# Scores on two 64-row tiles and outputs with sums on two 64-column tiles, in a windowed attention with sinks followed by a gated feed-forward layer

## The chip, the cores and the metric

The kernel runs on one core of a Trainium2 chip. The metric is device time in microseconds (us) of one execution. TensorE multiplies on a 128x128 array and writes PSUM, VectorE and ScalarE read PSUM and write SBUF, GpSimd (POOL) works in SBUF and issues some of the loads, SyncE (SP) issues the others.

## The reference

Four batches, eight heads, 768 positions, head width 64. Each query sees the first four positions (the sinks) and the last 128 up to itself. What follows is a gated feed-forward layer over the 512 values of a position.

```python
scores = scale * np.matmul(q, k.transpose(0, 1, 3, 2))
keep = is_sink | in_window            # pos < 4, or 0 <= rel < 128
scores = np.where(keep, scores, -1000000000.0)
a = np.exp(scores - np.max(scores, axis=-1, keepdims=True))
a = a / (np.sum(a, axis=-1, keepdims=True) + 1e-09)
attn = np.matmul(a, v)                # then x = attn as (3072, 512)
gate = np.maximum(x @ w_gate, 0.0)    # 512 -> 1536
out = (gate * (x @ w_val)) @ w_out    # 1536 -> 512
```

## The kernel before

**Attention.** A unit is a pair of heads (p = 0 to 3) of one batch. Keys are cut into blocks j of 124 positions; a block's 128 key columns are its 124 positions and the four sinks in front, so each block of keys meets a stretch of at most 255 queries. The steps of a unit: `load_kq` and `load_v` load k, q and v; `cast` turns k and q into bf16 on GpSimd (`kn`, `qn`); `T` transposes them on TensorE (`tk`, `tq` in PSUM) and copies the results to `kT` and `qz`. `qz` holds two copies of the queries with the other head's 64 rows zero, so that a 128-row matmul gives one head's scores. `S(gi)` makes the scores of a group of key blocks (`sps`), ScalarE takes the exponential into `ee`, VectorE multiplies with a 0/1 mask. `V(part, oab)` multiplies `ee` with `vn`, in which each head's 64 value columns have 64 columns of ones beside them: rows 0 to 63 of `ops` are the output, row 64 and those below it the sum of exponentials. ScalarE copies `ops` to `oab`.

**Normalisation.** Units of batches 1 to 3 (kind F, all 768 rows) go through `norm`: the sums leave by DMA to DRAM and come back as a 128x12 tile, VectorE takes the reciprocals some chunks later, these go to DRAM and come back as a broadcast `R` over 64 partitions, and again some chunks later VectorE multiplies `oab` by `R` into `xT` (`tick` counts the chunks). Batch 0 is cut into three kinds of units, A (252 rows), B (248) and C (268); they go through `norm0`, which transposes the sums out of PSUM on VectorE in 32x32 blocks, takes the reciprocal of one column per block and transposes back.

**Feed-forward.** `chunk(b, c0, n, m)` makes 128 of the 1,536 hidden values for n positions: four matmuls for the gate (`gp`), ScalarE's relu (`gs`), four for the values (`vp`), VectorE's product into `hT`. `ffn2` multiplies `hT` with `wo`, twelve matmuls of 512 columns per 128 positions, issued a few at a time behind later chunks. There are 108 chunks: 36 in batch 0 (three blocks) and 24 in each later batch (two blocks of 384).

**Order.** The order on every engine is the program order, written by hand. `unit_stages` lists the attention stages, `want` says how many of them stand ahead of a chunk. Two PSUM slots (`ps_at`) serve the transposes, scores and outputs in turn; three serve `gp` and `vp`, one serves `op`. Batch b's chunks need `xT` of all four units of that batch.

## Time and profile before

| what | value |
|---|---|
| time, median of 3 runs | 314.46 us (313.69 to 315.67) |
| the profiled execution | 312.14 us |
| its span, first to last instruction | 310.4 us |
| mean granted TensorE clock, share of 2.4 GHz | 0.984 |
| TensorE busy | 259.5 us (84%) |
| VectorE busy | 167.5 us (54%) |
| ScalarE busy | 163.2 us (53%) |
| GpSimd busy | 93.7 us (30%) |

Busy times are sums over all instructions of an engine; a share of the span is an average over stretches with different limits. In the rows below, a name with L and a number is a line of the kernel before; `x4` behind a group is its count of instructions; PEld is TensorE's weight load, which runs beside its matmuls.

### The profile page before, as it was taken

How to read it: one execution, taken by the hardware profiler on the slowest of the kernel's cores; microseconds unless marked ns; L12 is line 12 of the kernel's file. 1: busy time of each engine (PE TensorE's matmuls, PEld its weight loads, DVE VectorE, ACT ScalarE, POOL GpSimd, SP SyncE). 2: the span in 40 equal slices, each digit the busy share in tenths (PEclk: the TensorE clock that was granted, in tenths of full speed). 3: DMA queues.
4: the chain of work that ended last, by engine and by line, in shares of the span. 5: the costliest groups of instructions: out<-in, count | busy, mean ns of one | idle time of the engine just before them, and what ended most of it. 6: DMA issues, size and time to landing. Idle time of an engine off the chain costs nothing.

```text
span 310.4 us, 5251 instructions
## 1 busy us (share of the span) xinstructions
PE 259.5 (84%) x1868; PEld 168.2 (54%) x1868; DVE 167.5 (54%) x340; ACT 163.2 (53%) x300; POOL 93.7 (30%) x159
## 2 busy tenths in 40 slices
PE   1545856466798997749999999999999999999995
PEld 0333744354686765516666666666666555555552
DVE  4488667768765757544647473746454352222210
ACT  5553667445478875515566657565554333333321
POOL 7756247245595454230405050503000000000000
PEclk9999999989799999989999999999999999999999
DMA  5799997855898778391919373524312301000002
GB/s 134 140 219 202 222 236 128 130 116 117 128 151 133 186 88 145 85 201 46 171 63 188 68 150 85 64 85 29 87 36 88 84 35 37 34 34 36 34 34 101
DMA packets 55585, 33.75 MB, mean 109 GB/s; under 512 B 34428, under 2 KB 51708, under 8 KB 55560
## 3 DMA queue, kind: packets, MB, share of 16 engines
q1 hardware_dynamic: 25368, 25.59, 29.1%
q0 software_dynamic: 29104, 7.57, 24.8%
q10 hardware_dynamic: 1088, 0.26, 0.4%
q8 instruction: 14, 0.23, 0.3%
q14 instruction: 11, 0.09, 0.1%
HBM read 34.55 MB, written 6.44 MB: 132 GB/s over the span
## 4 chain that ended last, share of the span: by engine, by line
PE 55%; ACT 0%; issue 0%; ACTq 0%
PE op L411 18%; PE vp L398 15%; PE gp L392 15%; PE ops L248 3%; PE sps L232 3%; PE tk L188 1%; PE tq L195 1%; ACT ot L415 0%; ACTq L415 0%
## 5 line engine op out<-in xcount | busy, mean ns | idle before, releaser
L400 DVE TENSOR_TENSOR hT<-gs,vp 128x384 bf16<-128x384 f32 (+3 forms) x108 | 54.6, 506 | 72.2 <-PE vp L398 55.8
L392 PE MATMUL gp<-xT,wg 128*128 128x384 bf16 (+3 forms) x432 | 82.6, 315 | 4.5 <-DVE xT L364 4.5
L398 PE MATMUL vp<-xT,wv 128*128 128x384 bf16 (+3 forms) x432 | 82.7, 315 | 2.9 <-ACT gs L395 2.1
L411 PE MATMUL op<-wo,hT 128*128 128x512 bf16 x288 | 79.0, 383 | 0.0
L395 ACT ACTIVATE gs<-gp 128x384 f32<-128x384 f32 (+3 forms) x108 | 49.2, 455 | 41.2 <-PE gp L392 40.5
L398 PEld LDWEIGHTS <-wv 128*128 128x128 bf16 x432 | 43.3, 100 | 29.5 <-issue 8.6
L238 DVE TENSOR_TENSOR ee<-ee,msk 128x1006 bf16<-128x1006 bf16 (+6 forms) x52 | 38.6, 742 | 32.5 <-ACT ee L236 32.4
L236 ACT ACTIVATE ee<-sps 128x1006 bf16<-128x1006 f32 (+6 forms) x52 | 47.1, 906 | 14.7 <-PE sps L232 14.3
L392 PEld LDWEIGHTS <-wg 128*128 128x128 bf16 x432 | 40.1, 100 | 18.9
L151 POOL DMA_DIRECT2D vn<-in_v_dram x32 | 26.3, 825 | 71.8 <-PE ops L248 67.7
L411 PEld LDWEIGHTS <-hT 128*128 128x128 bf16 x288 | 28.4, 99 | 23.0 <-issue 0.6
L248 PE MATMUL ops<-ee,vn 128*128 128x248 bf16 (+9 forms) x264 | 28.2, 246 | 13.5 <-ACT qz L200 7.5
L248 PEld LDWEIGHTS <-vn 128*128 128x128 bf16 x264 | 22.6, 101 | 23.0 <-issue 13.8
L232 PE MATMUL sps<-qz,kT 128*128 128x251 bf16 (+6 forms) x136 | 27.5, 258 | 7.6 <-ACT qz L200 2.4
L252 ACT COPY oab<-ops 65x752 f32<-65x752 f32 (+1 forms) x24 | 19.0, 794 | 21.1 <-PE ops L248 21.0
L364 DVE TENSOR_TENSOR xT<-oab,R 64x768 bf16<-64x768 f32 x24 | 23.9, 996 | 11.2 <-DMA R<-rcp_tmp 10.9
L200 ACT COPY qz<-tq 64x768 bf16<-64x768 bf16 (+2 forms) x24 | 14.0, 584 | 24.8 <-DVE qz L200 24.6
L188 PE MATMUL tk<-ident,kn 128*128 128x128 bf16 (+2 forms) x112 | 11.5, 240 | 16.4 <-POOL kn L163 13.7
L232 PE MATMUL sps<-qz,kTs 128*128 128x248 bf16 (+3 forms) x104 | 25.0, 263 | 0.0
L415 ACT COPY ot<-op 128x512 f32<-128x512 f32 x24 | 14.0, 584 | 18.3 <-PE op L411 18.3
L191 ACT COPY kT<-tk 128x768 bf16<-128x768 bf16 (+3 forms) x24 | 15.1, 629 | 15.5 <-PE tk L188 15.4
L188 PEld LDWEIGHTS <-kn 128*128 128x128 bf16 (+2 forms) x112 | 8.7, 110 | 21.7 <-POOL kn L163 16.0
(61 smaller groups left out, 189.9 us busy)
## 6 DMA issues: line engine op xcount, KB each, us to landing
out_dram<-ot SPq DMA_DIRECT2D x24, 256.0 KB, 2.3
kf<-in_k_dram SPq DMA_DIRECT2D x24, 192.0 KB, 4.1
qf<-in_q_dram SPq DMA_DIRECT2D x24, 192.0 KB, 4.4
R<-rcp_tmp SPq DMA_DIRECT2D x12, 384.0 KB, 4.1
vn<-in_v_dram POOLq DMA_DIRECT2D x24, 96.0 KB, 3.6
wg<-in_moe_w_gate_dram POOLq DMA_DIRECT2D x4, 384.0 KB, 7.4
wv<-in_moe_w_val_dram POOLq DMA_DIRECT2D x4, 384.0 KB, 9.8
wo<-in_moe_w_out_dram POOLq DMA_DIRECT2D x3, 512.0 KB, 6.6
```

The costliest lines, as they stand in the source:

```text
L151: eng.dma_start(out=dst[:, o + j0:o + j0 + nj, h, 0:64], in_=bass.AP(src.tensor, src.offset + 124 * j0 * D, [[D, 128], [124 * D, nj], [1, ...
L188: nc.tensor.transpose(ps[:, t * kp:(t + 1) * kp], kn[s][0:kp, self.no + t, :, :].rearrange("p h d -> p (h d)"), ident[0:kp, 0:kp])
L232: nc.tensor.matmul(out=ps[:, h, c:c + w], lhsT=self.kw(j), rhs=qz[s][:, h, self.zo + qa:self.zo + qa + w], start=True, stop=True)
L236: nc.scalar.activation(x, ps[:, :, 0:c], Act.Exp, bias=0.0, scale=scale)
L238: nc.vector.tensor_tensor(x, x, bc(msk[:, m0:m0 + c], 2), op=Alu.mult)
L248: nc.tensor.matmul(out=ps[:, h, qa - q0:qa - q0 + w], lhsT=vn[s][:, self.vo + j, h, :], rhs=ee[s][:, gi, h, c:c + w], start=i == 0, stop=i ...
L364: nc.vector.tensor_tensor(xTs[b][64 * h:64 * h + 64, p, :], oab[0:64, h, :], R[:, h, :], op=Alu.mult)
L392: nc.tensor.matmul(out=gp[:, 0:n], lhsT=wg[:, ko, m * 128:(m + 1) * 128], rhs=x[:, ko, c0:c0 + n], start=ko == 0, stop=ko == KO - 1)
L395: nc.scalar.activation(gs[:, 0:n], gp[:, 0:n], Act.Relu, bias=0.0, scale=1.0)
L398: nc.tensor.matmul(out=vp[:, 0:n], lhsT=wv[:, ko, m * 128:(m + 1) * 128], rhs=x[:, ko, c0:c0 + n], start=ko == 0, stop=ko == KO - 1)
L400: nc.vector.tensor_tensor(hT[:, m, c0:c0 + n], gs[:, 0:n], vp[:, 0:n], op=Alu.mult)
L411: nc.tensor.matmul(out=op, lhsT=hTs[b][:, m, t * 128:(t + 1) * 128], rhs=wo[:, m, :], start=m == 0, stop=m == FM - 1)
```

## The change

- Scores: `qz` becomes `qT` with both heads' queries once. Head h's scores come from rows 64h to 64h+63 of the array, the two heads one behind the other in the order and into two PSUM banks.
- Outputs and sums: `ops` holds the outputs of head 0 in partitions 0 to 63 and of head 1 in 64 to 127, and the sums likewise in its other half. The sums come from matmuls with a tile of ones. All of these are 64 columns wide.
- Normalisation: every unit goes through one `norm`, like `norm0` before, and the product reads the output from PSUM. The DRAM round trip, the copies to `oab` and the counting of chunks are gone.
- Batch 0 has two kinds of units, L (376 rows) and M (392), and two blocks of chunks, so there are 96 chunks.
- Three staging buffers and three `vn`; one DMA for both heads of k or q; the sink rows of `vn` are copied by VectorE; `PLAN` replaces the numbers in `want`.

```diff
-    "A": dict(q0=0, n=252, ...),  "B": dict(q0=252, n=248, ...),  "C": dict(q0=500, n=268, ...)
+    "L": dict(q0=0, n=376, q=(0, 128, 3), k=(0, 96, 4), js=(0, 1, 2), sink=(1,),
+              groups=[[(0, 0, 255), (1, 128, 248)], [(2, 252, 132)]],
+              parts=[(0, 384, [(0, 0, 255), (1, 128, 248), (2, 252, 132)])]),
+    "M": dict(q0=376, n=392, q=(320, 112, 4), k=(208, 112, 5), js=(2, 3, 4, 5, 6), sink=(3, 5),
+              groups=[[(2, 352, 151), (3, 376, 248)], [(4, 500, 251), (5, 624, 144), (6, 748, 20)]],
+              parts=[(352, 416, [(2, 352, 151), (3, 376, 248), (4, 500, 251), (5, 624, 144), (6, 748, 20)])]),
...
-              parts=[(0, 376, [(0, 0, 255), (1, 128, 248), (2, 252, 124)]),
-                     (376, 392, [(2, 376, 127), (3, 376, 248), (4, 500, 251), (5, 624, 144), (6, 748, 20)])]),
+              parts=[(0, 384, [(0, 0, 255), (1, 128, 248), (2, 252, 132), (3, 376, 8)]),
+                     (384, 384, [(2, 384, 119), (3, 384, 240), (4, 500, 251), (5, 624, 144), (6, 748, 20)])]),
...
         def S(self, gi):
-            for h in range(2):
-                c = 0
-                for j, qa, w in self.groups[gi]:
-                    nc.tensor.matmul(out=ps[:, h, c:c + w], lhsT=self.kw(j),
-                                     rhs=qz[s][:, h, self.zo + qa:self.zo + qa + w], start=True, stop=True)
+            for j, qa, w in self.groups[gi]:
+                for h in range(2):
+                    r = slice(64 * h, 64 * h + 64)
+                    nc.tensor.matmul(out=ps[:, h, c:c + w], lhsT=self.kw(j, r), rhs=qT[s][r, qa:qa + w],
+                                     start=True, stop=True)
...
-        def V(self, part, oab):
-            for h in range(2):
+        def V(self, part):
+            for what in range(2):
                 for i, (j, qa, w) in enumerate(segs):
...
-                    nc.tensor.matmul(out=ps[:, h, qa - q0:qa - q0 + w], lhsT=vn[s][:, self.vo + j, h, :],
-                                     rhs=ee[s][:, gi, h, c:c + w], ...)
-            if self.kind == "F":
-                nc.scalar.copy(oab[0:65, :, q0:q0 + n], ps[0:65, :, 0:n])
+                    for h in range(2):
+                        nc.tensor.matmul(out=ps[64 * h:64 * h + 64, 1 - what, qa - q0:qa - q0 + w],
+                                         lhsT=self.vn[:, j, h, :] if what else ones[:],
+                                         rhs=ee[s][:, gi, h, c:c + w], ...)
...
+    def norm(u, part):
+        ps = u.V(part)
+        r = rpool.tile([128, 2, 416], F32, name="R")
+        nc.vector.transpose(r[:, 0, 0:w], ps[:, 1, 0:w])
+        nc.vector.reciprocal(rc[:, 0:nb], r[:, 0, 0:w].rearrange("p (b j) -> p b j", j=32)[:, :, 0])
+        nc.vector.transpose(r[:, 1, 0:w], bass.AP(a.tensor, a.offset, [a.ap[0], [1, nb], [0, 32]]))
+        nc.vector.tensor_tensor(xTs[u.b][:, u.p, lo:hi], ps[:, 0, lo - c0:hi - c0], r[:, 1, lo - c0:hi - c0], op=Alu.mult)
...
+            if u.kind == "M":
+                return [s(0), v, t, s(1)]
+            return [s(0), v, s(1), t, s(2), lambda: norm(u, 0)]
...
-        blocks = [(0, 0, 252), (0, 252, 248), (0, 500, 268)]
+        blocks = [(0, 0, 376), (0, 376, 392)]
...
+        PLAN = ((0, 0), (3, 0), (12, 19), (23, 43), (47, 67), (71, 89), (72, 90))
```

Three places of the order. TensorE, the first half of a full unit's outputs, before: 128 columns wide, one head after the other.

```order
L248 LDWEIGHTS vn_93
L248 MATMUL ops<-ee_103,vn_93 128x127
L248 LDWEIGHTS vn_93
L248 MATMUL ops<-ee_103,vn_93 128x248
L248 LDWEIGHTS vn_93
L248 MATMUL ops<-ee_103,vn_93 128x251
```

And a half now: 64 wide, the two heads in turn, first the sums with the ones and then the outputs with `vn`.

```order
L231 LDWEIGHTS ones
L231 MATMUL ops<-ee_101,ones 64x119
L231 LDWEIGHTS ones
L231 MATMUL ops<-ee_101,ones 64x119
...
L231 LDWEIGHTS vn_92
L231 MATMUL ops<-ee_101,vn_92 64x119
L231 LDWEIGHTS vn_92
L231 MATMUL ops<-ee_101,vn_92 64x119
```

Ten matmuls of such a second half have become twenty. TensorE, around the first chunk of batch 0's last block, now (392 columns; its `xT` comes from the outputs just ahead of it):

```order
L213 MATMUL sps<-qT_100,kT_96 128x20
L213 LDWEIGHTS kT_95
L213 MATMUL sps<-qT_99,kT_95 128x255
...
L231 LDWEIGHTS vn_91
L231 MATMUL ops<-ee_102,vn_91 64x20
L305 LDWEIGHTS wg
L305 MATMUL gp<-xT,wg 128x392
```

Nothing stands between the last outputs of batch 0 and the chunk that needs them. Before, the first chunk of batch 1 stood behind a score group, and the outputs that it needs behind several chunks ahead of it:

```order
L411 MATMUL op<-wo,hT 128x512
L232 LDWEIGHTS kT_98
L232 MATMUL sps<-qz_102,kT_98 128x251
...
L392 LDWEIGHTS wg
L392 MATMUL gp<-xT,wg 128x384
```

VectorE, a piece of one full unit of batch 1, before:

```order
L238 TENSOR_TENSOR ee_104<-ee_104,msk 128x2x503
L400 TENSOR_TENSOR hT<-gs,vp 128x268
L364 TENSOR_TENSOR xT<-oab_106,R 64x768 x2
L355 RECIPROCAL dr<-dc 128x12
L238 TENSOR_TENSOR ee_104<-ee_104,msk 128x2x499
```

And now, from the end of one unit to the start of the next:

```order
L160 COPY vn_92<-vn_92 4x3x128
L290 STREAM_TRANSPOSE R<-ops 128x384
L291 RECIPROCAL rc<-R 128x12
L293 STREAM_TRANSPOSE R<-rc 128x384
L295 TENSOR_TENSOR xT<-ops,R 128x384
L313 TENSOR_TENSOR hT<-gs,vp 128x392
L219 TENSOR_TENSOR ee_102<-ee_102,msk 128x2x503
L290 STREAM_TRANSPOSE R<-ops 128x384
```

The two 64-row products of the normalisation have become one per half, with two transposes and a reciprocal ahead of each, and they stand directly among masks and chunk products.

## Rows read from the trace of the kernel before

**Rows 1.** Stretches: start:end, length, busy us of each engine (instructions), clock, DMA share, GB/s.
```profile
core 0: us, PE busy (x) PEld busy (x) DVE busy (x) ACT busy (x) POOL busy (x), PEclk, DMA share, GB/s
0.00:26.54 26.54, 10.87 (x67) 6.77 (x68) 16.82 (x45) 14.82 (x32) 19.03 (x52) 1.00 0.84 166
26.54:78.64 52.10, 32.77 (x297) 25.00 (x296) 37.83 (x95) 28.70 (x69) 24.66 (x42) 0.97 0.90 164
78.64:131.55 52.91, 45.05 (x410) 35.38 (x407) 34.52 (x66) 36.55 (x60) 26.87 (x35) 0.97 0.75 130
131.55:136.68 5.13, 0.65 (x5) 0.29 (x3) 1.92 (x3) 1.26 (x2) 2.42 (x4) 0.99 1.37 241
136.68:142.00 5.32, 5.32 (x30) 2.98 (x30) 2.78 (x6) 1.68 (x3) 0.50 (x1) 0.69 0.19 69
142.00:246.47 104.47, 104.47 (x740) 65.43 (x738) 56.74 (x100) 61.10 (x99) 20.27 (x28) 1.00 0.43 88
```

**Rows 2.** Waits of TensorE: engine, line, releaser: us in total, times, longest us.
```profile
PE tk L188 <- POOL kn L163: 13.7, 6, 4.2
PE ops L248 <- ACT qz L200: 7.5, 7, 1.9
PE gp L392 <- DVE xT L364: 4.5, 1, 4.5
```

**Rows 3.** Order of time, TensorE, dense part: start us, us, operation, shapes, count.
```profile
169.53 0.50 PE L188 MATMUL tk<-ident,kn 128*128 128x128 bf16 x6
...
170.20 0.81 PE L392 MATMUL gp<-xT,wg 128*128 128x384 bf16 x4
...
172.14 0.27 PE L232 MATMUL sps<-qz,kT 128*128 128x251 bf16 x1
...
172.45 0.22 PE L232 MATMUL sps<-qz,kTs 128*128 128x144 bf16 x1
...
172.54 0.81 PE L392 MATMUL gp<-xT,wg 128*128 128x384 bf16 x4
...
174.48 0.71 PE L248 MATMUL ops<-ee,vn 128*128 128x255 bf16 x6
175.03 0.81 PE L392 MATMUL gp<-xT,wg 128*128 128x384 bf16 x4
```

**Rows 4.** Groups by line and shape, VectorE: busy us, mean ns of one, idle time before.
```profile
L400 DVE TENSOR_TENSOR hT<-gs,vp 128x384 bf16<-128x384 f32 x72 | 39.7, 552 | 62.5 <-PE vp L398 54.7 <-PE sps L232 6.7 <-POOL vn L176 0.9
L238 DVE TENSOR_TENSOR ee<-ee,msk 128x998 bf16<-128x998 bf16 x12 | 10.6, 885 | 9.9 <-ACT ee L236 9.9
L238 DVE TENSOR_TENSOR ee<-ee,msk 128x1006 bf16<-128x1006 bf16 x12 | 8.2, 686 | 12.3 <-ACT ee L236 12.3
L238 DVE TENSOR_TENSOR ee<-ee,msk 128x830 bf16<-128x830 bf16 x12 | 8.0, 662 | 7.4 <-ACT ee L236 7.4
L375 DVE STREAM_TRANSPOSE R<-ops 64x288 f32<-64x288 f32 x8 | 3.9, 485 | 2.8 <-ACT oab L255 2.7
L355 DVE RECIPROCAL dr<-dc 128x12 f32<-128x12 f32 x12 | 2.7, 223 | 0.1
L378 DVE STREAM_TRANSPOSE R<-rc 128x288 f32<-128x288 f32 x4 | 1.9, 478 | 0.1
```

**Rows 5.** Order of time at the start, VectorE's normalisations and TensorE's first chunk.
```profile
15.63 0.92 DVE L375 STREAM_TRANSPOSE R<-ops 64x256 f32<-64x256 f32 x2 [1.28 <-ACT oab L255]
...
26.71 0.42 DVE L382 TENSOR_TENSOR xT<-oab,R 128x252 bf16<-128x252 f32 x1
...
26.54 1.05 PE L392 MATMUL gp<-xT,wg 128*128 128x252 bf16 x4
27.38 1.05 PE L398 MATMUL vp<-xT,wv 128*128 128x252 bf16 x4
```

**Rows 6.** Groups by line and shape, ScalarE.
```profile
L236 ACT ACTIVATE ee<-sps 128x830 bf16<-128x830 f32 x12 | 10.4, 869 | 1.4 <-PE sps L232 1.2
L191 ACT COPY kT<-tk 128x768 bf16<-128x768 bf16 x12 | 9.6, 799 | 9.4 <-PE tk L188 9.3
```

**Rows 7.** Groups by line, TensorE's weight loads of the value weights.
```profile
L398 PEld LDWEIGHTS <-wv 128*128 128x128 bf16 x432 | 43.3, 100 | 29.5 <-issue 8.6
```

More of the change, by code (lines that the diff above doesn't have):

```diff
@@ L95 @@
     wo = const.tile([128, FM, d_model], BF16, name="wo")
+    ones = const.tile([128, 64], BF16, name="ones")
     ident = const.tile([128, 128], BF16, name="ident")
@@ L243, in V @@
             ps = ps_at.tile([128, 2, 512], F32, name="ops", tag="at")
-            for h in range(2):
+            for what in range(2):
                 for i, (j, qa, w) in enumerate(segs):
@@ L315, in setup_m1 @@
         cp(msk[:, 1397:1417], band(0, 20))
[L317 to L340 removed]
     xTs = {}
     ready = {}
[L345 to L375 removed]
+    def norm(u, part):
+        c0, w = u.parts[part][0:2]
+        nb = w // 32
+        lo, hi = (max(c0, u.q0), min(c0 + w, u.q0 + u.n))
+        ps = u.V(part)
+        r = rpool.tile([128, 2, 416], F32, name="R")
+        rc = dpool.tile([128, 13], F32, name="rc")
+        nc.vector.transpose(r[:, 0, 0:w], ps[:, 1, 0:w])
         nc.vector.reciprocal(rc[:, 0:nb], r[:, 0, 0:w].rearrange("p (b j) -> p b j", j=32)[:, :, 0])
@@ L378, in norm0 @@
         nc.vector.transpose(r[:, 1, 0:w], bass.AP(a.tensor, a.offset, [a.ap[0], [1, nb], [0, 32]]))
-        busy.discard(next(i for i in range(4) if oab_[i] is oab))
-        ready[0, u.p] = u.q0 + u.n
-        o = u.q0 - c0
-        nc.vector.tensor_tensor(xTs[0][:, u.p, u.q0:u.q0 + u.n], oab[:, 0, o:o + u.n], r[:, 1, o:o + u.n], op=Alu.mult)
+        ready[u.b, u.p] = hi
+        nc.vector.tensor_tensor(xTs[u.b][:, u.p, lo:hi], ps[:, 0, lo - c0:hi - c0], r[:, 1, lo - c0:hi - c0], op=Alu.mult)
     hTs = {}
@@ L450, in casts @@
                 u.cast(w, nc.gpsimd)
-        def V0(p):
-            o = new_oab()
-            norm0(A[p], o, A[p].V(0, o))
-        casts(A[0], "kqv")
+        for p in range(3):
+            U[p].load_kq(nc.sync)
+            U[p].load_v(nc.scalar if p == 0 else nc.sync)
+        setup_pool()
+        nc.scalar.activation(ee[0][:, 0, 0, 0:128], ident[:], Act.Exp, bias=0.0, scale=1.0)
+        setup_slot(0)
+        for s in range(3):
+            nc.vector.memset(vn[s][:, 6, :, :], 0.0)
+        nc.vector.memset(ones[:], 1.0)
@@ L457, with next_load @@
+        xTs[0] = xpool.tile([128, NP, S], BF16, name="xT")
+        hTs[0] = hpool.tile([128, FM, S], BF16, name="hT", tag="hT")
+        def next_load(x):
+            w = at(x + 3)
+            if w is not None:
+                w.load_kq(nc.sync)
+                if w.kind == "L":
+                    w.load_v(nc.sync)
+        casts(U[0], "kqv")
+        next_load(0)
         setup_m0()
-        A[0].T(*GV)
+        U[0].T(*GV)
         setup_slot(1)
-        casts(A[1], "kqv")
-        A[1].T(*GV)
+        casts(U[1], "kqv")
@@ L462 @@
+        next_load(1)
+        U[1].T(*GV)
         for p in range(NP):
-            A[p].S(0)
+            for gi in range(2):
+                U[p].S(gi)
             if p + 2 < NP:
-                casts(A[p + 2], "kqv")
+                casts(U[p + 2], "kq" if p else "kqv")
+                U[p + 2].T(*GV)
                 if p == 0:
-                    load_w(0)
-                A[p + 2].T(*GV)
-            if p == 2:
-                casts(rest[0], "kq")
-            if p == 3:
-                rest[0].T(*GV)
@@ L484 @@
+            if p >= 2:
+                casts(U[p + 2], "kq")
+                next_load(p + 2)
+                load_w(p)
+        norm(U[NP - 1], 0)
+        U[6].load_v(nc.gpsimd)
         setup_m1()
         stages = []
-        opart = {}
-        def V_(u, part):
-            last = part == len(u.parts) - 1
-            if part == 0:
-                opart[u.i] = new_oab()
-            ps = u.V(part, opart[u.i])
-            if last and u.kind == "F":
-                norm(u, opart.pop(u.i))
-            elif last:
-                norm0(u, opart.pop(u.i), ps)
@@ L510, in f @@
                     u.S(gi)
[L511 to L518 removed]
+                    if gi == len(u.groups) - 1:
+                        u.sinkv(nc.vector)
+                        if at(x + 2) is not None and x > NP:
+                            at(x + 2).load_v(nc.gpsimd)
@@ L520, in v @@
+                return f
             def v():
-                if prev is not None:
-                    V_(prev, len(prev.parts) - 1)
-                    if nxt is not None:
-                        if nxt.kind == "B":
-                            casts(nxt, "v")
-                        else:
-                            nxt.load_v(nc.gpsimd, False)
-                if kind != "F":
-                    prefetch()
+                if x > NP:
+                    norm(prev, len(prev.parts) - 1)
```

267 lines of the change are left out of this document (70 added, 197 removed).

## Prediction, made before the changed kernel ran

> **What bounds the kernel now.** I read three views, in this order. First the table of stretches [rows 1], cut where the work changes. From 136.68 us on TensorE is busy in every microsecond until the last output tile is copied: 5.32 of 5.32, then 104.47 of 104.47. In that dense part only TensorE work counts, and VectorE (56.74 of 104.47) and ScalarE (61.10) have room. Ahead of it TensorE is busy for 10.87 of 26.54, 32.77 of 52.10, 45.05 of 52.91 and 0.65 of 5.13 us. This front part is a chain of hand-overs, and what it waits for is in the waits of TensorE [rows 2]: key casts at the start (13.7 us), PSUM slots that the query copies hold (7.5 us), and one single wait of 4.5 us for the normalised xT of batch 1, which came by four DMAs through DRAM. So I cost the change in two parts, split where the first chunk of batch 1 begins (136.68 us). Before, they are 136.7 and 173.7 us, together the span of 310.4; the profiled execution took 312.14, so 1.74 lie around the span. The median of the timed runs, 314.46, is 2.3 above it. I carry both over.
>
> **Rates from the dense part** [rows 3]. A chunk of eight 384-column matmuls and three 512-column ones runs from 170.20 to 172.14, 1.94 us for 4,608 columns: 2.4 GHz gives 1.92, so some 2 ns per matmul on top. The group with 251, 144 and 20 columns per head takes 0.40 (172.14 to 172.54), an output part of six 0.55 (174.48 to 175.03), the twelve transposes of a unit 0.67 (169.53 to 170.20). For a full unit (1,417 columns and two heads, 1.18 us, plus 3 to 5 ns for each of 14 to 16 matmuls) that makes 1.26 for scores and 1.28 for outputs.
>
> **The dense part after the change.**
> - *Counts.* The order shows, behind the first batch-1 chunk, 6.5 units of scores, 7 of outputs and 6 of transposes before, and 7.5, 8 and 7 after, since that chunk now comes earlier among the attention stages.
> - *Scores.* Two heads on two 64-row tiles. If the two stream side by side a unit needs 1,417 column times, 0.59, with overheads 0.63; if not, 1.26. No row shows two tiles at work. I take 0.79, a speed-up of 1.6 of 2.
> - *Outputs and sums.* Sums are now matmuls of their own, so 5,668 columns in 36 matmuls. Side by side that is 1.18 plus overhead, 1.28; one after the other 2.36 plus overhead, 2.47. Many matmuls are short, and each has its weight load: the pair of 144 and 20 columns ends 0.09 after it began (172.45 to 172.54), so a load and its matmul can follow at 45 ns. 36 times 45 ns are 1.6 us. I take 1.60.
> - *Sum.* Before 6.5 x 1.26 + 7 x 1.28 + 6 x 0.67 = 21.2; after 7.5 x 0.79 + 8 x 1.60 + 7 x 0.67 = 23.4: +2.2.
> - *Output rows left over.* Batch 0 now ends in a block of 392 rows, so 48 instead of 36 second-layer matmuls follow in batch 1: 12 x 512 / 2.4 = +2.6.
> - *Changing the tile shape.* The change alternates 128-row, 64-row and 64-column matmuls; the order has 137 changes of shape, 76 of them here. No row has one. The lower bound is nothing. For the upper I take what a matmul's record lasts beyond its pace: 0.27 us for 251 columns (the row at 172.14), which at 2.4 GHz stream in 0.105, so 0.16. I take 0.05, nearer to nothing, since transposes and matmuls alternate in these rows with no gap: 76 x 0.05 = +3.8. The Trainium skill, TensorEngine Tiling (Array Packing), Key Properties, says that changing the tiling mode drains the TensorE; no run here shows it, and it is the rule that speaks most against this change, so the third rival prices a drain from the rows.
> - *Clock.* After the 4.5 us wait the granted clock was 0.69 for 5.32 us [rows 1], with 1.2 GHz in part of it: 0.31 x 5.32 = 1.6 us lost. That wait goes (the reciprocals stay on chip), so -1.6; with 0.5 that three matmuls had run before the wait, +0.5.
>
> Sum: 173.7 - 1.6 + 0.5 + 2.2 + 2.6 + 3.8 = 181.2. Bounds: 173.6 (side by side, no cost of a shape change), 201 (one after the other, 0.16 each).
>
> Is TensorE still the bound there? VectorE per full unit [rows 4]: masks 0.885 + 0.686 + 0.662 = 2.23; the two key copies and the sink rows of V, now on VectorE, some 0.7; per half a transpose of 384 columns from PSUM (0.485 for 288, plus 96 at 1.03 ns = 0.585), reciprocal 0.223, transpose back 0.58, product 0.552: 1.94, twice 3.9; together 6.8. With six chunk products of 0.552 that is 10.1 against at least 14 us of TensorE work: covered.
>
> **The front part after the change.** Here 8 units instead of 12 and 24 chunks instead of 36 stand, so widths grow and hand-overs shrink.
> - *Start.* The last stretch of the start is VectorE's: four normalisations with masks between them, 15.63 to 27.13, 11.5 us, and the first chunk begins at 26.54 [rows 5]. After: four of 1.97, two pairs of masks of 1.0 and hand-overs of 1.3, 11.2 us, beginning about 1.2 us later since units are 376 instead of 252 rows wide: first chunk at 28.0. If the start scaled with the width, 15.63 x 1.5 would give 34; not below 26.5.
> - *Four chunks with no attention between.* A first layer half-chunk at 1.2 GHz takes 0.84 for 252 columns (26.54 to 27.38), so two cold chunks of 376 make 5.0 and two warm ones 2.6: 35.6.
> - *Four M units, two chunks each.* The output's PSUM slot is now held until VectorE has done four steps (2.0), not a ScalarE copy, and with two slots the second transpose tile of the unit after waits for it. TensorE work 4.3 (chunks 2.5, scores 0.5, outputs 0.9, nine transposes 0.4) plus some 1.9 of that wait: 6.2, above VectorE's 5.1 (masks 1.3, copies 0.7, normalisation 2.0, products 1.1). Four make 24.8: 60.4.
> - *Chunk 12* follows directly on the last M unit's exponential (0.87 [rows 6]), mask (0.66 [rows 4]), output matmuls and normalisation (2.0), with a second exponential and mask between: about 5 us with an idle TensorE, and 1.6 of low clock after it, as before at 131.55: 67.0. This is the old wait in a new place.
> - *Four full units of batch 1, three chunks each.* VectorE needs 6.8 + 3 x 0.55 = 8.5 per unit, TensorE 5.2 (three chunks of 4,160 columns) + 0.8 + 1.6 + 0.7 = 8.3, and both halves' normalisations follow each other through the same two slots. VectorE waits once per unit for ScalarE's two copies (0.80 for keys, the like for queries) and the next exponential (0.87) [rows 6], of which a product and the key copies cover about 1.0: 10.0 per unit, 107.0. Fully packed it would be 8.5; at the share that VectorE reached in this stretch before (34.52 of 52.91), 13.1.
> - *Last unit*: two normalisations in a row ahead of chunk 23: +2.0, 109.0.
>
> Bounds: 93 (26.5, one cold chunk, 5.1 and 8.5 per unit, waits of 4 and 1) and 129 (34, 6.5 and 13.1 per unit, waits of 7 and 3). The removed DMAs (48 through DRAM, and the 384 KB broadcasts) and the casts cost nothing now except in the waits named; GpSimd loses the sink copies and keeps its loads.
>
> **Sum.** 109.0 + 181.2 + 1.74 = 291.9 against 312.14, and with the 2.3 by which the median stands above the profiled execution, 294 us. The front gives 27.7, the dense part takes back 7.5.
>
> **Rivals.**
> - *Front shorter than I think* (VectorE packed, start not later): 109 - 4 x 1.1 - 4 x 1.5 - 1.5 = 97, and with tiles side by side and 0.02 a change of shape 175 for the dense part: 97 + 175 + 4 = 276. For it: fewer hand-overs per row. Against: the start was never packed before.
> - *The tiles don't run side by side*, so the change doesn't do what it says: outputs +0.87 a unit (x 8), scores +0.47 (x 7.5): +10.5; in the front up to 9, of which some 6 lies beside VectorE's chain or waits: 294 + 17 = 311. If that holds for columns alone, 294 + 7 + 4 = 305. For it: nothing in the rows, which have no tiles. Against: a load and matmul at 45 ns shows that the next weights are loaded while the array streams. The Trainium skill, TensorE: Matmul & The Clock Gate, Part 3 (The mechanism), says that weight loads overlap running matmuls only when their row group differs, which two column tiles don't have; the trace disagrees already for 128-row matmuls, whose loads hide behind their predecessors, so I give it little.
> - *A change of shape empties the array, on the slow side.* The next matmul would wait for the last record's end (0.16) and load its weights only then (0.10 [rows 7]): 0.26. 76 x 0.21 above my 0.05 is 16, and half of the 61 in the front 6: 316. Slower than before from 0.25 a change on. For it: the chain is long, 137 changes. Against: mixed transposes without a gap.
>
> **How the numbers follow.** Forecast (277 to 303) 0.65; shorter front (below 277) 0.08; no side by side (303 to 313) 0.15; shape changes and whatever else lies above 313, 0.12. The range 276 to 312 leaves out 0.07 below and 0.13 above. About 1% is what a measurement of this kernel can tell from no change. Faster by over 1% (below 311.3): 0.65 + 0.08 + most of the 0.15 = 0.86; within: 0.07; slower by over 1% (above 317.6): 0.07.
>
> **What would show it.** First chunk near 28; the first 384-column chunk near 109; a wait of about 5 us ahead of chunk 12; output parts of 0.7 to 0.9 in the dense part (1.2 if one after the other); no wait of TensorE behind 115. Wrong would be a dense part of 195 or more, output parts of over 1.2, a granted clock well below 1.00 there, or a front of over 125.

## The result, and the profile after

| | before | after |
|---|---|---|
| time, median | 314.07 us (312.22 to 315.67) | 289.67 us (288.47 to 290.86) |
| profiled execution, its span | 312.14, 310.4 us | 288.47, 286.8 us |
| first 384-column chunk (ready and running) | 136.68 us | 104.58 us |
| from there to the end | 173.7 us | 182.2 us |

The medians are of four executions each; the profile of before is the one that the prediction used. The ratio is 0.9225 (95% interval 0.916 to 0.9289): 7.7% faster. 294.0 was predicted, with a range of 276 to 312. The front gave 32.1 us (27.7 predicted), and the dense part took back 8.5 (7.5 predicted).

The stretches of after, cut at the places that the prediction named (columns as in [rows 1]):

```profile
core 0: us, PE busy (x) PEld busy (x) DVE busy (x) ACT busy (x) POOL busy (x), PEclk, DMA share, GB/s
0.00:27.46 27.46, 13.24 (x103) 7.64 (x104) 15.20 (x44) 11.27 (x22) 22.24 (x47) 1.00 1.15 232
27.46:33.78 6.32, 6.32 (x29) 3.38 (x29) 2.65 (x7) 1.89 (x4) 4.30 (x7) 1.00 1.40 240
33.78:59.97 26.19, 20.60 (x238) 13.29 (x236) 21.49 (x44) 16.83 (x28) 16.07 (x22) 1.00 1.33 239
59.97:62.32 2.35, 0.68 (x8) 0.31 (x5) 2.19 (x5) 0.00 (x0) 2.02 (x3) 1.00 1.14 312
62.32:104.58 42.26, 35.85 (x370) 21.38 (x369) 32.70 (x67) 23.16 (x34) 16.04 (x21) 1.00 0.51 84
104.58:222.90 118.32, 118.32 (x961) 65.81 (x960) 71.20 (x147) 57.75 (x95) 20.02 (x26) 1.00 0.31 60
```

They are: the start until the last product that the first chunk needs; the four chunks without attention; the four M units; the wait of chunk 12; the four full units of batch 1; and most of the dense part, where TensorE is again busy in every microsecond (118.32 of 118.32). The clock column reads 1.00 in every stretch, where before had 0.69 for 5.32 us [rows 1]. For the four chunks it does not tell all. TensorE in order of time there:

```profile
28.98 1.46 PE L305 MATMUL gp<-xT,wg 128*128 128x376 bf16 x4
30.24 1.16 PE L311 MATMUL vp<-xT,wv 128*128 128x376 bf16 x4
```

Four matmuls of 376 columns take 1.25 us from 28.98 (1.2 GHz), 0.99 from 30.24, and 0.64 from 31.23 on (2.4 GHz). So the clock rose some 31 us into the span, although the column has 1.00 from the start. Below, a matmul at 1.2 GHz is called cold.

The waits of TensorE (total us, times, longest):

```profile
PE tk L172 <- POOL kn L149: 9.1, 4, 4.6
PE gp L305 <- DVE xT L295: 3.5, 3, 1.7
PE sps L213 <- ACT ee L217: 2.6, 3, 1.1
PE ops L231 <- DVE vn L160: 2.5, 2, 1.2
PE tq L179 <- ACT kT L175: 2.3, 3, 0.9
```

Against [rows 2]: the key casts take 9.1 us in four waits, instead of 13.7 in six. The 7.5 us that outputs waited on `qz` are gone. The single wait of 4.5 for `xT`, ahead of batch 1, is gone; of the three that are left two stand at the very first chunk (0.36 and 1.48) and the longest, 1.67, ahead of chunk 12. New is a wait for VectorE's sink-row copies (2.5).

TensorE in order of time, one unit's last score group and first output half in the dense part:

```profile
141.80 0.81 PE L324 MATMUL op<-wo,hT 128*128 128x512 bf16 x3
142.54 0.28 PE L213 MATMUL sps<-qT,kT 64*128 64x251 bf16 x2
142.66 0.23 PE L213 MATMUL sps<-qT,kTs 64*128 64x144 bf16 x2
142.72 0.18 PE L213 MATMUL sps<-qT,kT 64*128 64x20 bf16 x2
142.83 0.82 PE L305 MATMUL gp<-xT,wg 128*128 128x384 bf16 x4
...
144.14 0.81 PE L324 MATMUL op<-wo,hT 128*128 128x512 bf16 x3
144.88 0.47 PE L231 MATMUL ops<-ee,ones 128*64 128x255 bf16 x8
145.21 0.45 PE L231 MATMUL ops<-ee,vn 128*64 128x255 bf16 x8
145.60 0.82 PE L305 MATMUL gp<-xT,wg 128*128 128x384 bf16 x4
```

Three second-layer matmuls stream 512 columns each, 0.64 us at 2.4 GHz, so the ones from 141.80 end at 142.44. The score group of 415 columns per head begins 0.10 later, at 142.54. From 142.44 to the next chunk at 142.83 it takes 0.39; before, the same group took 0.40 [rows 3]. The output half takes 0.82 (144.78 to 145.60), and before 0.55 [rows 3]. So the tiles brought the dense part nothing for scores and a loss for outputs. What they do inside their 0.39 and 0.82 the experiments had to tell.

VectorE's copies of the sink keys, as a group (busy us, mean ns of one):

```profile
L199 DVE COPY kTs<-kT 128x12 bf16<-128x12 bf16 x12 | 7.3, 612 | 0.0
```

The mean hides two lengths. Two of the twelve in order of time, the first with a GpSimd cast beside it, the second with none:

```profile
141.23 0.88 POOL L149 CAST qn<-stg 128x768 bf16<-128x768 f32 x1
141.40 0.73 DVE L199 COPY kTs<-kT 128x12 bf16<-128x12 bf16 x1
...
189.57 0.15 DVE L199 COPY kTs<-kT 128x12 bf16<-128x12 bf16 x1
```

Eight stand beside a cast of `qn` and take 0.73 or 0.74, one beside a cast of `kn` takes 1.04 (at 56.65), and the three with no cast beside them take 0.15.

### The profile page after: what moved, and what is told of

Same layout as the page of the kernel before. It is cut to its first block, busy times and chain, and to the rows that moved or that the text cites. A ratio compares the mean times of both kernels' runs of the same rounds, so it can differ in the third digit from the quotient of the medians.

```text
span 286.8 us, 5306 instructions
## 1 busy us (share of the span) xinstructions
PE 255.2 (89%) x2056; PEld 144.4 (50%) x2056; DVE 164.2 (57%) x347; ACT 130.3 (45%) x218; POOL 80.7 (28%) x123
## 4 chain that ended last, share of the span: by engine, by line
PE 80%; DVE 8%; ACT 4%; DMA 3%; issue 2%; POOL 1%; SPq 0%; ACTq 0%; POOLq 0%
PE gp L305 23%; PE op L324 22%; PE vp L311 21%; PE ops L231 7%; PE sps L213 4%; ACT ee L217 3%; DMA stg<-in_q_dram 3%; PE tk L172 2%; DVE R L293 2%; DVE xT L295 2%; DVE R L290 2%; PE tq L179 2%; DVE ee L219 1%; ACT kT L175 1%; DVE kTs L199 1%
## 5 line engine op out<-in xcount | busy, mean ns | idle before, releaser
L305 PE MATMUL gp<-xT,wg 128*128 128x384 bf16 (+2 forms) x384 | 80.4, 331 | 3.5 <-DVE xT L295 3.5
L308 ACT ACTIVATE gs<-gp 128x384 f32<-128x384 f32 (+2 forms) x96 | 47.3, 493 | 78.5 <-PE gp L305 77.1
L311 PE MATMUL vp<-xT,wv 128*128 128x384 bf16 (+2 forms) x384 | 79.1, 329 | 0.0
L313 DVE TENSOR_TENSOR hT<-gs,vp 128x384 bf16<-128x384 f32 (+2 forms) x96 | 52.5, 547 | 42.5 <-PE vp L311 40.0
L217 ACT ACTIVATE ee<-sps 128x1006 bf16<-128x1006 f32 (+4 forms) x52 | 46.6, 906 | 32.0 <-PE sps L213 32.0
L219 DVE TENSOR_TENSOR ee<-ee,msk 128x1006 bf16<-128x1006 bf16 (+4 forms) x52 | 33.7, 655 | 34.1 <-ACT ee L217 34.0
L290 DVE STREAM_TRANSPOSE R<-ops 128x384 f32<-128x384 f32 (+1 forms) x32 | 18.7, 586 | 14.6 <-PE ops L231 14.6
L231 PE MATMUL ops<-ee,ones 128*64 128x144 bf16 (+9 forms) x280 | 17.6, 250 | 2.6 <-ACT ee L217 1.7
L231 PEld LDWEIGHTS <-ones 128*64 128x64 bf16 x280 | 13.0, 112 | 13.7 <-issue 9.3
L293 DVE STREAM_TRANSPOSE R<-rc 128x384 f32<-128x384 f32 (+1 forms) x32 | 18.6, 583 | 1.1
L295 DVE TENSOR_TENSOR xT<-ops,R 128x384 bf16<-128x384 f32 (+2 forms) x32 | 17.8, 558 | 1.1
```

The costliest lines, as they stand in the source:

```text
L217: nc.scalar.activation(x, ps[:, :, 0:c], Act.Exp, bias=0.0, scale=scale)
L219: nc.vector.tensor_tensor(x, x, bc(msk[:, m0:m0 + c], 2), op=Alu.mult)
L231: nc.tensor.matmul(out=ps[64 * h:64 * h + 64, 1 - what, qa - q0:qa - q0 + w], lhsT=self.vn[:, j, h, :] if what else ones[:], rhs=ee[s][:, ...
L290: nc.vector.transpose(r[:, 0, 0:w], ps[:, 1, 0:w])
L293: nc.vector.transpose(r[:, 1, 0:w], bass.AP(a.tensor, a.offset, [a.ap[0], [1, nb], [0, 32]]))
L305: nc.tensor.matmul(out=gp[:, 0:n], lhsT=wg[:, ko, m * 128:(m + 1) * 128], rhs=x[:, ko, c0:c0 + n], start=ko == 0, stop=ko == KO - 1)
```

## The experiments

Each kernel stands with its span and the start of its first 384-column chunk (the front), in one profiled execution. "Median" stands where four or more executions were timed; every other time is a single execution.

| kernel | front | dense part | span | time |
|---|---|---|---|---|
| after | 104.58 | 182.2 | 286.8 | 289.67 median |
| sw_128 | 104.54 | 184.0 | 288.6 | 290.26 |
| sw_row | 104.65 | 191.3 | 296.0 | 297.66 |
| sw_col | 105.76 | 193.0 | 298.7 | 300.44 |
| s_serial | 106.87 | 182.3 | 289.2 | 290.85 |
| v_serial | 105.18 | 183.0 | 288.2 | 289.88 |
| s_full | 110.66 | 182.2 | 292.9 | 294.56 |
| v_full | 109.58 | 179.7 | 289.3 | 290.98 |
| no_tiles | 124.27 | 180.7 | 304.9 | 304.12 median |
| before | 136.68 | 173.7 | 310.4 | 314.07 median |
| before_norm | 143.1 | 179.6 | 322.7 | 324.53 |
| v_full_late | 105.40 | 179.7 | 285.1 | 287.21 median |
| late_plan | 104.63 | 179.7 | 284.3 | 286.97 median |
| late_pair | 107.39 | 182.2 | 289.6 | 291.19 median |

### What one change of the tile's shape costs

One small matmul of 8 columns is put ahead of each of the 72 chunks of batches 1 to 3, in three shapes. Its result lands in columns that nobody reads.

```diff
         gp = ps_gv.tile([128, 512], F32, name="gp", tag="gv")
+        if b >= 1:   # sw_128: 128 rows, 128 columns
+            nc.tensor.matmul(out=gp[:, 400:408], lhsT=wg[:, 0, 0:128], rhs=x[:, 0, 0:8], start=True, stop=True)
+                     # sw_row: lhsT=wg[0:64, 0, 0:128], rhs=x[0:64, 0, 0:8]
+                     # sw_col: out=gp[0:64, 400:408], lhsT=wg[:, 0, 0:64]
```

> The changed kernel with one more matmul of 8 columns, 128 rows and 128 columns wide like its neighbours, ahead of each of the 72 chunks of batches 1 to 3 (its result is not used). It is the control for the next two. Both theories: 0.03 to 0.045 us each, 2 to 3 us in all, the profiled span goes from 286.8 to 289 to 290.

> The same extra matmul, but on 64 rows, so 144 changes of the tile shape more than the control. My theory: a change costs about 0.095 us (the gaps around score groups in the profile after), so 144 x 0.095 = 14 us above the control, 303. Rival, a change costs nothing and the gaps are weight loads of the groups themselves: as the control, 289 to 290. Rival, a full drain and reload of 0.26: 37 us above the control.

> The same extra matmul, but 64 columns wide. My theory: as for 64 rows, about 0.09 a change, 13 us above the control. Rival, nothing: as the control. Rival, column tiles cost more than row tiles (their weight loads are slower): over 0.12 a change, 17 us or more above the control.

The span grew by 1.8 us with the 128-row matmul, by 9.2 with 64 rows and by 11.9 with 64 columns. TensorE in order of time, at a chunk that stands directly behind another one, in sw_128:

```profile
254.67 0.81 PE L326 MATMUL op<-wo,hT 128*128 128x512 bf16 x3
255.31 0.17 PE L305 MATMUL gp<-xT,wg 128*128 128x8 bf16 x1
255.34 0.81 PE L307 MATMUL gp<-xT,wg 128*128 128x384 bf16 x4
```

in sw_row:

```profile
255.65 0.81 PE L326 MATMUL op<-wo,hT 128*128 128x512 bf16 x3
256.39 0.18 PE L305 MATMUL gp<-xT,wg 64*128 64x8 bf16 x1
256.50 0.82 PE L307 MATMUL gp<-xT,wg 128*128 128x384 bf16 x4
```

and in sw_col:

```profile
256.08 0.81 PE L326 MATMUL op<-wo,hT 128*128 128x512 bf16 x3
256.82 0.19 PE L305 MATMUL gp<-xT,wg 128*64 128x8 bf16 x1
256.95 0.82 PE L307 MATMUL gp<-xT,wg 128*128 128x384 bf16 x4
```

From the first `op` to the first `gp` it is 0.67, 0.85 and 0.87. So the two changes cost 0.18 and 0.20 over the control, some 0.10 each, half on the way in (0.74 instead of 0.64 from `op`) and half on the way out.

The spans grew by less than 72 times 0.19. Sorting all chunks but the first by what stands ahead of them explains it. From the starts of the chunks, behind a 128-row piece (33 chunks) a 64-row insertion costs 0.19 over the control and a 64-column one 0.20. Behind a score group (22) they cost -0.02 and 0.10, and behind an output half (16) 0.08 and 0.00. A matmul of the shape that is already set costs nothing, and one of the other shape costs one change more. 33 x 0.19 + 16 x 0.08 - 22 x 0.02 = 7.1 against 7.3 measured between the dense parts of sw_row and sw_128, and 33 x 0.20 + 22 x 0.10 = 8.8 against 9.0 for sw_col.

The price of a change is thus 0.10 us. It is twice the 0.05 that was taken, and under half of the 0.25 from which the kernel would have been slower. The Trainium skill, TensorEngine Tiling (Array Packing), Key Properties, says that a change of the tiling mode, and not of the tile alone, drains TensorE. The trace agrees that a change costs time and that staying within a shape does not (-0.02 and 0.00); the Trainium skill names no price. Whether the 0.10 us are the array running empty is not shown, since the ends of matmul records are modelled. A weight load that no longer hides would cost as much: a load lasts 0.10 [rows 7], and the first one of a score group begins only together with its matmul (both at 144.87 in s_serial).

### Do the two tiles run side by side, and does it need heads in turn?

s_serial writes a group's scores head by head, v_serial a half's sums and outputs head by head. All else is as in after.

```diff
-            for j, qa, w in self.groups[gi]:          # s_serial
-                for h in range(2):
+            for h in range(2):
+                for j, qa, w in self.groups[gi]:
...
-                for i, (j, qa, w) in enumerate(segs):  # v_serial
-                    for h in range(2):
+                for h in range(2):
+                    for i, (j, qa, w) in enumerate(segs):
```

> The changed kernel with the scores of head 0 first and then those of head 1, so neighbours are on the same row tile. My theory (row tiles stream side by side only as neighbours): about 0.55 us more per full unit, +4 us in the dense part and about 2 in front, span 291 to 293. Rival (overlap in any order): 286 to 288.

> The changed kernel with the outputs and sums in another order: all blocks of head 0, then all of head 1, so neighbours in the order are on the same column tile. My theory (two column tiles stream side by side when their matmuls are neighbours): a full unit's outputs go from 1.75 to some 2.7 us with the gaps, +7 us in the dense part and 2 to 4 in front of it, span 296 to 298. Rival (the two tiles overlap in any order, or the short time has another reason): unchanged, 286 to 288.

The dense parts are 182.3 and 183.0 against 182.2. TensorE in order of time, the 415-column group in s_serial:

```profile
144.87 0.29 PE L213 MATMUL sps<-qT,kT 64*128 64x251 bf16 x2
144.99 0.23 PE L213 MATMUL sps<-qT,kTs 64*128 64x144 bf16 x2
145.05 0.18 PE L213 MATMUL sps<-qT,kT 64*128 64x20 bf16 x2
145.17 0.82 PE L305 MATMUL gp<-xT,wg 128*128 128x384 bf16 x4
```

and an output half in v_serial:

```profile
145.69 0.48 PE L231 MATMUL ops<-ee,ones 128*64 128x255 bf16 x8
146.02 0.48 PE L231 MATMUL ops<-ee,vn 128*64 128x255 bf16 x8
```

The program lists 251, 144 and 20 columns of head 0 and then the three of head 1. The records start two of 251 columns together at 144.87, two of 144 at 144.99 and two of 20 at 145.05. Each width occurs once per head, so one of each two is head 1's. The group lasts 0.30 as in after (0.29), which holds 0.17 for 415 columns at 2.4 GHz and 0.10 for the change behind it. So two tiles do stream at the same time, and the order within a stage does not decide it. The theory that neighbours in the order have to belong to different tiles falls. In v_serial eight matmuls take 0.33, as in after, for 643 columns per head (0.27 at 2.4 GHz): column tiles stream side by side too. There the order is not quite free: with short pieces, a unit's second half takes 1.00 us in v_serial instead of 0.92, and its first 0.83 instead of 0.81, which over the eight units makes the 0.8 by which the dense part is longer. The Trainium skill, TensorEngine Tiling (Array Packing), Key Properties, says that tiles operate independently: the trace agrees. The Trainium skill, TensorE: Matmul & The Clock Gate, Part 3, says that matmuls start strictly in program order, and that a load overlaps running matmuls only in another row group. Here the measurements differ from both: head 1's 251 columns start ahead of head 0's 144, and the eight loads of column tiles, which share all their rows, fit into the 0.33 us.

s_serial's 2.4 us more lie in the front, and 1.4 of them in the clock. Its wait ahead of chunk 12 is the same 1.67, but what follows is not. First the stretch behind it in s_serial, then in after:

```profile
63.00:68.00 5.00, 3.90 (x24) 1.92 (x25) 1.25 (x3) 2.16 (x4) 1.18 (x2) 0.67 0.66 57
```

```profile
62.30:67.00 4.70, 4.03 (x32) 2.30 (x32) 2.30 (x4) 3.29 (x5) 1.99 (x3) 1.00 0.74 64
```

The granted clock is 0.67 in the one and 1.00 in the other, with the same work ahead of it. Chunk 12 and what stands with it take 6.9 us (60.8 to 67.7) instead of 5.5 (60.0 to 65.5). The timed executions of after show both: mean clock 1.000 with spans of 286.8 and 287.9, and 0.992 and 0.993 with 288.1 and 289.2, 1.3 us more on average. Where the clock was low in these two, their means do not tell.

### What the tiles are worth

s_full takes scores on 128 rows again: queries of both heads padded with zeros, which ScalarE copies in two pieces. v_full takes outputs and sums of batches 1 to 3 in one 128-column matmul per block and head; ScalarE copies the outputs out of PSUM, and the division stays on chip. no_tiles does both, for batch 0 as well.

```diff
-                    nc.tensor.matmul(out=ps[:, h, c:c + w], lhsT=self.kw(j, r), rhs=qT[s][r, qa:qa + w],   # s_full
+                    nc.tensor.matmul(out=ps[:, h, c:c + w], lhsT=self.kw(j, slice(0, 128)), rhs=qz[s][:, h, qa:qa + w],
...
+            if self.full:                                                                                 # v_full
+                        nc.tensor.matmul(out=ps[:, h, qa - q0:qa - q0 + w], lhsT=self.vn[:, j, h, :],
+                                         rhs=ee[s][:, gi, h, c:c + w], ...)   # vn: 64 columns and 64 ones
...
+                nc.scalar.copy(oab[64 * h:64 * h + 64, 0:w], ps[0:64, h, 0:w])
```

> The changed kernel with the scores as before: 128-row matmuls on queries with the other head's rows zero, so ScalarE copies the queries twice. My theory (what two row tiles save, 0.6 us per unit, goes into the two changes of shape around each of the three score groups): the dense part stays within 1 us of 182.2, the span is 286 to 291 with the second copy in front. Rival (row tiles pay, as my prediction had it with 0.79 us per unit): the dense part is 3 us or more longer, the span 291 to 294.

> The changed kernel with the outputs of batches 1 to 3 as before: 128 columns wide, 64 of V and 64 of ones, no tile of ones and no changes of shape; ScalarE copies the outputs and VectorE transposes the sums in two pieces, as batch 0 did before. My theory (column tiles with separate sums lose 0.45 us a unit against this): the dense part 3 to 4 us shorter (178 to 179), the front 2 to 5 us longer since VectorE does 1.2 us more per unit, span 286 to 290. Rival (column tiles pay or cost nothing): the dense part 182 or more, span 288 to 293.

> The changed kernel without any tile of the array: scores are 128 rows deep on queries padded with zeros (ScalarE copies the queries twice), outputs and sums 128 columns wide in all units (ScalarE copies the outputs out of PSUM). What stays of the change is the division on chip, batch 0 in two halves instead of three blocks, and the loads. Theory (the gain is the front's, and there the two halves carry it; the tiles only spare ScalarE its copies): padded queries alone gave +6.1 in the front and 128-column outputs of batch 1 alone +5.0; with some 2 for the outputs of batch 0 the first chunk of batch 1 begins at 104.6 + 13 = 118, the dense part stays at 179.7 (as in the run with 128-column outputs), so a span of 298, 300 us as a median, still 4% below the kernel before. Rival (the tiles carry the front; the kernel before with the division on chip and three blocks had its first chunk of batch 1 at 143): front 130 or more, span 310 or more, no gain over the kernel before.

TensorE in order of time, the group of 503 columns per head in s_full:

```profile
201.00 0.81 PE L328 MATMUL op<-wo,hT 128*128 128x512 bf16 x3
201.65 0.38 PE L215 MATMUL sps<-qz,kT 128*128 128x255 bf16 x2
201.87 0.38 PE L215 MATMUL sps<-qz,kTs 128*128 128x248 bf16 x2
202.08 0.81 PE L309 MATMUL gp<-xT,wg 128*128 128x384 bf16 x4
```

and the first output half in v_full:

```profile
148.93 0.75 PE L233 MATMUL ops<-ee,vn 128*128 128x255 bf16 x8
149.53 0.81 PE L323 MATMUL gp<-xT,wg 128*128 128x384 bf16 x4
```

From the end of `op` (201.64) the full-height group takes 0.44; the tiled one in after takes 0.42. The dense parts are equal, 182.2 and 182.2. The output half takes 0.60 instead of 0.82, and the dense part is 2.5 us shorter. So in the dense part row tiles are worth nothing, and column tiles with sums of their own cost.

In the front it is the reverse. Without row tiles it is 6.1 us longer, without column tiles in batch 1 5.0, without any 19.7. Of the 6.1 some 1.5 are the clock: behind the same wait of 1.7 us chunk 12 is cold, as in s_serial, and takes 7.0 us to the next chunk (62.29 to 69.28) instead of 5.5. So s_full's span, 292.9, missed its expected 286 to 291 in the front alone. TensorE's order of time and its clock around chunk 12 in no_tiles:

```profile
71.53 0.49 PE L327 MATMUL gp<-xT,wg 128*128 128x392 bf16 x1 [3.47 <-DVE xT L317]
```

```profile
67.40:76.70 9.30, 5.37 (x30) 3.19 (x29) 3.96 (x8) 3.15 (x5) 3.10 (x4) 0.63 0.35 23
120.00:124.30 4.30, 4.30 (x18) 2.12 (x16) 3.78 (x8) 2.03 (x4) 2.05 (x3) 0.50 0.75 47
```

The chains through ScalarE's copies and VectorE grow, the wait ahead of chunk 12 doubles to 3.47, and the clock falls to 0.63 and later to 0.50. In the first stretch 4.7 us of TensorE's work stand behind the wait, at half speed; in the second all of its 4.30 do. So the low clock costs at most half of that, 2.4 + 2.2 = 4.5 us, of the 6.3 that separate 124.3 from the 118 of the theory that adds the parts; how much of it other engines' work hides was not measured. The rival's 130 is not reached either: the ratio to before is 0.97 (0.966 to 0.9741). The profiled execution (306.75) is 2.6 longer than the median. So of the 32.1 us that the front gained, 12 (by the median some 15) are left without tiles, and the larger part came with them. Without them the chains are longer again, and the mean clock is lower: 0.947 to 0.989 in the five executions of no_tiles, 0.992 to 1.000 in the four of after. What carries the rest was not separated: the two halves of batch 0 and the new loads were not tried alone, and no_tiles keeps the order that was written for the tiles.

### The division on chip alone

before_norm is the kernel before, whose full units divide by VectorE transposes from PSUM as batch 0 does; their two parts are cut at 384. Batch 0 stays in three blocks, without tiles.

```diff
-            if last and u.kind == "F":
-                norm(u, opart.pop(u.i))
-            elif last:
-                norm0(u, opart.pop(u.i), ps)
+            o = new_oab()
+            norm0(u, o, u.V(part, o), part)
```

> The kernel before with one part of the change alone: units of batches 1 to 3 are divided on chip by VectorE transposes, halves of 384, like batch 0, with no DRAM trip. My theory (this takes away the one wait of 4.5 us and the low clock behind it, and loads VectorE more): span 303 to 308 from 310.4, the wait ahead of the first chunk of batch 1 under 2 us. Rival (the DRAM trip is what makes the front long): span under 298. Rival (VectorE becomes the bound in the front): 310 or more.

It is slower, 324.53 against 312.93 of before beside it, one execution each, and the expected span of 303 to 308 fell. The wait of 4.5 for `xT` is gone, but its 143.1 for the front is 6.4 more than before's; there the outputs' waits for query copies grew from 7.5 us to 12.2, and from 26.3 to 79.7 us the clock is 0.90 where it was 0.97 [rows 1]. The waits of TensorE behind 143 us, where before had TensorE busy throughout:

```profile
PE vp L395 <- ACT gs L392: 2.4, 3, 0.9
PE gp L389 <- DVE hT L397: 2.2, 2, 1.3
PE vp L395 <- DVE hT L397: 1.8, 5, 0.5
```

They add up to 6.4 us, the size of the 5.9 by which the dense part grew: ScalarE and VectorE run late. VectorE is busy for 199.0 us instead of 167.5, since the two heads' sums lie in two PSUM banks and it transposes each head's for itself. Alone, the division on chip does not pay.

### Three candidates

v_full_late is v_full with the 128-column outputs in batches 2 and 3 alone, whose attention lies in the dense part. late_plan adds an earlier table for the second half of batch 0. late_pair adds to that one unit's second and third score group side by side.

```diff
+            self.full = kind == "F" and b >= 2                                                  # v_full_late
...
-        PLAN = ((0, 0), (3, 0), (12, 19), (23, 43), (47, 67), (71, 89), (72, 90))
+        PLAN = ((0, 0), (2, 0), (11, 19), (23, 43), (47, 67), (71, 89), (72, 90))                 # late_plan
...
-            return [s(0), v, s(1), t, s(2), lambda: norm(u, 0)]
+            return [s(0), v, t, lambda: None, pair, lambda: norm(u, 0)]    # late_pair, batches 2 and 3; pair: s(1), s(2)
```

> The changed kernel, but the units of batches 2 and 3 (not those of batch 1) take outputs and sums in one 128-column matmul per key block and head, as the kernel before did; ScalarE copies the outputs out of PSUM, and VectorE divides as in the changed kernel. These eight units have their outputs in the dense part. Theory (the column tiles lose in the dense part, since each half pays two changes of shape of 0.10 us and twice the matmuls): a unit's two halves take 0.60 + 0.71 = 1.31 us, as in the run where batch 1 had them too, instead of 0.815 + 0.93 = 1.745, so 8 x 0.43 = 3.5 us less in the dense part (2.5 less were measured when batch 1 did the same), and the front stays at 104.6 because nothing in it differs: span 283.3 to 284.3, about 287 us as a median. Rival (the copies hold PSUM slots, and ScalarE's four copies a unit delay its exponentials, so TensorE now waits in the dense part): dense part no shorter than 182, span 286 to 289.

> The kernel with 128-column outputs in batches 2 and 3, and the table of stages begins one chunk earlier for the second half of batch 0, so that its last outputs are normalised one chunk ahead of the chunk that needs them (chunk 12). Theory (the 1.7 us wait ahead of chunk 12 is a matter of order): that wait goes, span 1 to 1.7 us shorter than with the table unchanged, about 282. Rival (the front is a chain of hand-overs, VectorE's and the two PSUM slots', and not a matter of where a chunk stands): the waits ahead of the earlier units grow by what chunk 12 saves, front within 0.5 us of the same.

> As the one with the earlier table, and in batches 2 and 3 the second and third score group of a unit stand directly behind each other. Theory (a change of shape costs 0.10 us wherever it stands, and two groups of one shape side by side share theirs): two changes fewer per unit, 8 x 0.20 = 1.6 us less than the one with the earlier table alone, all in the dense part. Rival (the exponentials of both groups then come late for the next user of the two PSUM slots): new waits of TensorE in the dense part, 0 to 2 us more.

**v_full_late** has a median of 287.21 us (286.85 to 287.5), ratio 0.9131 (0.9059 to 0.9202) to before; all its executions are faster than all of after (288.47 to 290.86). Its dense part is 179.7, 2.5 below after, as v_full had, and not the 3.5 that the halves' lengths give: to 230 us TensorE's records leave 1.4 us uncovered (123.25 of 124.60, where after has none), 0.6 of it a wait for an `xT`.

**late_plan** has 286.97 (286.04 to 287.43), the same within the spread. Its front is 0.8 shorter in the profile, but the two are already 1.2 apart at the end of the third chunk (32.17 against 33.34), up to which the table changes nothing: there the clock rose earlier. The wait of 1.7 ahead of chunk 12 is gone, but waits for sink rows rose from 2.5 to 5.0, and those of key transposes for a unit's `xT` from 0.8 to 3.1. The rival held: the front is a chain, and moving its chunks does not shorten it.

**late_pair** has 291.19 (290.95 to 292.33): slower. The pair itself works as expected. TensorE in order of time:

```profile
208.97 0.81 PE L342 MATMUL op<-wo,hT 128*128 128x512 bf16 x3
209.72 0.28 PE L215 MATMUL sps<-qT,kT 64*128 64x251 bf16 x2
...
210.22 0.82 PE L323 MATMUL gp<-xT,wg 128*128 128x384 bf16 x4
...
212.94 0.65 PE L233 MATMUL ops<-ee,vn 128*128 128x248 bf16 x7 [0.49 <-DVE vn L162]
```

Both groups take 0.61 from the end of `op` at 209.61, where in after the two take 0.42 and 0.39: two changes of shape are saved. But the next output half stands one chunk behind the last mask, and waits 0.49 for the sink rows of `vn`, which VectorE copies only behind that mask (2.3 us over six units). The chunks with the transposes, which now follow the division directly, take 2.85 instead of 2.63. So in such a unit 0.2 was won and 0.7 lost. The eight units' dense part is 2.5 longer than late_plan's, more than these terms make together (2.3 of waits and five longer chunks at 0.22, less 1.6); the rest is not traced. Its front is 2.8 longer: 1.3 at the end of the third chunk (33.48 against 32.17), most of it by a later rise of the clock, the rest by a unit's transposes (0.8 of it a wait) that now stand ahead of the first 384-column chunk.

## Why the prediction was right

It was 4.3 us too high. The front was 4.4 too long, the dense part 1.0 too short, and the median stands 1.2 above the profiled execution instead of 2.3 (the sum was 294.2 before rounding). Behind the sums some terms were wrong.

**The front, 109.0 predicted and 104.58 measured.**

| step | predicted | measured |
|---|---|---|
| start, to a first chunk that can run | 28.0 | 27.46 |
| four chunks | 7.6 | 6.3 |
| four M units | 24.8 | 26.2 |
| ahead of chunk 12, low clock included | 6.6 | 2.35 |
| four units of batch 1, the last one longer | 42.0 | 42.3 |

The start and batch 1 (10.0 per unit plus 2) were right to 0.5 us.

The **M units** came within 1.4 us by luck. Per unit 4.3 us of TensorE work were expected and 1.9 of waiting until the division frees a PSUM slot. TensorE was busy for 20.60 us there, 5.2 per unit, and idle for 5.6 in all, and no wait in the stretch is put down to the division. They are those of `tq` for ScalarE's key copy (2.3), of scores for VectorE's and ScalarE's copies (1.3 and 1.0) and of outputs for exponentials and masks (0.9).

The step that failed most is **chunk 12**. 5 us with an idle TensorE were expected, and 1.6 of low clock behind it. The exponential and the mask of the last unit cost only 0.9 us of idle time, inside the M units' stretch, since the score group and the first output matmuls stand beside them; and three quarters of the first matmuls needed only older products. What is left is a wait of 1.67 with three matmuls ahead of it. The low clock did not come in this execution, but came in s_serial and s_full behind the same wait, and two of the four executions of after show as much in their mean clock. So the term of 1.6 exists, but not in every execution.

In the **four chunks** three of the first chunk's matmuls had run ahead of the stretch (0.9 us at 1.2 GHz), and the clock rose inside the second chunk instead of behind it.

**The dense part, 181.2 predicted and 182.2 measured.** Two terms were mis-sized, in opposite directions:

- *Changes of shape:* 0.05 taken, 0.10 measured. 76 of them are 7.6 instead of 3.8. The upper bound of 0.16, from the records' length beyond their pace, held. The argument for a value nearer to nothing (transposes and matmuls alternate without a gap) was wrong: all of those are 128 rows by 128 columns, so no shape changes there.
- *Tiles:* a unit's scores were put at 0.79. Without the changes around its three groups (six, 0.6) they take 0.62, of the full side by side of 0.63. Outputs and sums were put at 1.60, and take 0.62 + 0.73 = 1.35 without their four changes, near the 1.28 of side by side. 7.5 x 0.17 + 8 x 0.25 = 3.3 us less.

Together the error is 0.5, and that they nearly cancel is luck; the other half of the 1.0 is not traced. So a unit's scores cost 1.22 with their changes (1.26 before) and its outputs 1.75 (1.28 before): the whole speed of the tiles went into the changes of shape, and the doubled matmuls for sums came on top.

**VectorE hidden in the dense part:** right, with no wait of TensorE from 104.58 to 222.90. The key copies and sink rows were put at 0.7 per unit and take 0.36 + 0.61 + 0.27 = 1.24 in the mean. With no GpSimd cast beside them they are 0.29 + 0.15 + 0.27 = 0.71; what the term left out is the cast beside them.

**Bounds.** By its own terms the dense part's upper bound is 200 and not 201, and the front's are 92 and 130 and not 93 and 129. The forecast does not hang on them.

**Rivals.** Tiles one after the other: fell, for rows and for columns. A change that empties the array at 0.25 or more: a change does cost time, but 0.10. A shorter front: right in direction (4.4 of 12 us). That ScalarE or VectorE becomes the bound was not among the rivals; it shows in before_norm and no_tiles, where waits for their copies and products grow.

## What to carry to other kernels

Count the changes of tile shape before the columns saved: at 0.10 us each, a stage of less than 480 columns per tile with 128-row work on both sides (two changes, 0.20 us at 2.4 GHz) gains nothing from two tiles. Stages of one shape should stand side by side only where what waits for them is not pushed later. Where TensorE is not the bound, tiles may still pay through the copies and chains that they spare other engines, and through shorter waits, behind which the clock fell less often here. Cost front and dense part apart, and check a predicted wait against what already lies beside it.

## What was not expected of the hardware

- Matmuls of different tiles start together even where the program lists one tile's matmuls ahead of the other's (both 251-column ones at 144.87 in s_serial).
- A change between 128x128 and a tile shape costs 0.10 us on each side, and an added matmul of 8 columns without one 0.025 (1.8 us for 72).
- The same wait of 1.67 us is followed by a granted clock of 0.67 in one execution and of 1.00 in another.
- A copy of 128x12 on VectorE takes 0.15 us alone and 0.73 beside a GpSimd cast (eight of twelve; one takes 1.04). The wider copy ahead of it, 128x372, takes 0.29 alone (189.36) and 0.90 beside a cast at 65.91.
